# Parting dependent VectorE operations in the kernel stage of an S4 convolution, and the skip term's sum on GpSimd

## The chip, the cores and the metric

One Trainium2 chip, one of its NeuronCores. A core has five engines with a queue each: TensorE (PE, matrix products), VectorE (DVE), ScalarE (ACT), GpSimd (POOL) and SyncE (SP, which here only issues DMAs). Engines run side by side and wait for one another through semaphores. The metric is the device time of one execution in microseconds (us); lower is better.

## The reference

The model has two blocks, each run twice: a state-space convolution (S4) with a residual, and a SwiGLU feed-forward network with a residual. Length 2048, width 512, state size 128, inner width 1376, all in float32.

```python
dt = jnp.exp(log_dt)[:, None]
logdA = dt * (A_re + 1j * A_im)
dB = dt * (B_re + 1j * B_im)
P = jnp.exp(logdA[:, :, None] * l[None, None, :])      # l = 0 .. 2047
K = jnp.einsum("dn,dnl,dn->dl", Cc, P, dB).real        # convolution kernel, 512 x 2048
y = irfft(rfft(pad(K)) * rfft(pad(u)))[:L] + u * Dskip
...
x = x + S4(layernorm(x));  x = x + (silu(n @ w_gate) * (n @ w_up)) @ w_down, n = layernorm(x)
# both again, with the same weights
```

## The kernel before, in words

Work starts with the **kernel stage**: the convolution kernel K is built for 512 channels in eight chunks of 64 (`NCH = 8`, `DC = 64`). The state index lies on the 128 partitions. A lag l is written as 64 b + a, and its power as a product of two tables: `re`, `im` (the factors over a) and `g` (over b, 32 steps, with the weights C, B and dt multiplied in). PE multiplies both tables and sums over the states: these are the *lags* (`lags`, L509 and L510), 64 small products for each chunk.

For a chunk the steps are these, each written as a Python generator that yields between pieces:

- `gen_turns` (L402 to L412, VectorE): phases as integers. L402 makes those of `xz`, L406 and four L410 double up those of `im[:, 33:65]`; at the end GpSimd clears `im[:, 32]` (L412).
- `gen_trig` (ACT): sines and cosines of them, into `xz`, `re[:, 33:65]` and `im[:, 33:65]`. `gen_exp` (ACT): magnitudes, with a memset of `re[:, 0]` by GpSimd (L435). `upper` (ACT, L443): squares of `re[:, 1:32]` into `mu`.
- `gen_e` (VectorE): magnitude times phase: L457 for `im[:, :32]`, L459 for `re[:, :32]`, L461 for `im[:, 33:64]`, L464 twice for the two halves of `re[:, 33:64]`.
- `gen_g` (VectorE): L471, L475/L476 and L478/L479 make `g[0]`; then a chain of doublings for n = 1, 2, 4, 8, 16. Each is a product with the real part (L485), a product with the imaginary part into a scratch tile (L496) and their sum (L499). L496 doesn't need L485; L499 needs both; the next L485 needs L499. For n = 16 in the middle chunks L488 writes the second product into the unused half of the next chunk's `g`, and a DMA from GpSimd's queue (L489) adds it to `g` in place of L499.

After the lags ACT copies them (L520), two DMAs from SP's queue turn them around (`spread`, L527 and L529, into the tile `kt`), and `skip` (L516) adds the chunk's 64 values of Dskip to one row of `kt`, which is the skip term of the convolution. PE then takes the spectra of `kt` (`spectra`, L544, in two halves q0 = 0 and 1; ACT reads them at L563 to L568, VectorE at L572), and the result goes to DRAM as `wdr` and to the tile `w0r`. Between them PE also transforms the input's second block (L309) and sums the weights' squares (L349), which ACT makes at L346.

The tiles `re` and `im` have two buffers in turn: chunk c + 2 uses those of chunk c. `g` has two as well, `mu` and the scratch tile one.

Order: VectorE, ACT, PE and GpSimd each run their instructions in the order in which the code issues them. The first chunk's order is written out by hand (`take(gg, 1)` takes the next piece of a generator). For the others a plan holds entries `at(due, piece, n)`; it is sorted by `due`, and so gives one order for all engines. The due times are no clock: only their order counts. In period i, with start t, the plan holds `use(i, t)` (lags, copy, skip, spectra of chunk i), `factors(i + 1, t)` (`gen_g` and `gen_e` of the next chunk) and `prepare(i + 2, t)` (turns, exponentials and sines of the one after). The last chunk has an order of its own behind the plan, in which its `skip` is on GpSimd already.

After the kernel stage the convolutions by blocks (`ssm`) and the feed-forward blocks (`ffn`) follow until the end.

Of the kernel before, what the change touches and what calls it, by code (L numbers as in the profile page):

```python
# [16 lines left out]
OP = mybir.AluOpType  # L17
# [16 lines left out]
NCH = D // DC  # L34
# [41 lines left out]
def kernel(ctx, tc, x, a_re, a_im, b_re, b_im, c_re, c_im, log_dt, d_skip,  # L76
                           w_gate, w_up, w_down, c_ef, c_ei, c_ek, c_am, c_eh, c_eih, out):
    nc = tc.nc
    V, A, G, PE = nc.vector, nc.scalar, nc.gpsimd, nc.tensor
# [9 lines left out]
    def tl(shape, name, tag, dt=F32):  # L89
        return sb.tile(shape, dt, name=name, tag=tag, bufs=BUFS[tag])  # L90
# [38 lines left out]
    x1 = tl([P, 4, D], "x1", "xf")  # L129
# [70 lines left out]
    def stats(src, rows, scale, tag="stats", then=None):  # L200

        st = tl([P, 4, 6], "st", tag)
        mv = tl([P, 4, 2], "mv", tag)
        rs = tl([P, 8], "rs", tag)
        nb = rs[:, 4:]
        for r in range(rows):
            V.bn_stats(st[:, r], src[:, r])
            V.bn_aggr(mv[:, r], st[:, r])
        V.tensor_scalar(rs[:, :rows], mv[:, :rows, 1], EPS, 1.0 / scale ** 2, OP.add, OP.mult)
        G.tensor_tensor(rs[:, :rows], rs[:, :rows], mhalf[:, :rows], OP.pow)  # L210
        if then:
            then()
        V.scalar_tensor_tensor(nb[:, :rows], mv[:, :rows, 0], -1.0, rs[:, :rows], OP.mult, OP.mult)
        return rs, nb
# [160 lines left out]
    def gen_tiles(ch):  # L375
        re = tl([P, 65, DC], "re", f"W{2 * (ch % 2)}")
        im = tl([P, 65, DC], "im", f"W{2 * (ch % 2) + 1}")
        mu = tl([P, 32, DC], "mu", "n")
        xz = tl([P, 3, 5, DC], "xz", "bd")
        mz = mz2[:, ch % 2]  # L380
        return re, im, mu, xz, mz
# [70 lines left out]
    def gen_e(ts):  # L452


        re, im, mu = ts[:3]
        half = [[t.rearrange("p a (g h d) -> p a g h d", g=4, h=2)[:, :, :, o] for t in (re, mu)] for o in range(2)]
        V.tensor_tensor(im[:, :32], im[:, 64:32:-1], re[:, :32], OP.mult)  # L457
        yield
        V.tensor_tensor(re[:, :32], re[:, 64:32:-1], re[:, :32], OP.mult)  # L459
        yield  # L460
        V.scalar_tensor_tensor(im[:, 33:64], im[:, 31:0:-1], -1.0, mu[:, 1:], OP.mult, OP.mult)  # L461
        yield
        for r, u in half:
            V.tensor_tensor(r[:, 33:64], r[:, 31:0:-1], u[:, 1:], OP.mult)  # L464
            yield

    def gen_g(ch, ts, g):

        re, im, mu, xz, mz = ts
        w_ = w0[:, :, ch * DC:(ch + 1) * DC]  # L470
        V.tensor_tensor(xz, xz, mz.unsqueeze(1).to_broadcast([P, 3, 5, DC]), OP.mult)  # L471
        yield
        tmp8 = spare[0][:, :16 * DC].rearrange("p (i b d) -> p i b d", i=2, d=DC)
        tmp = tmp8
        V.tensor_tensor(g[:, :, 0], w_, re[:, 64].unsqueeze(1).to_broadcast([P, 2, DC]), OP.mult)  # L475
        V.tensor_tensor(tmp[:, :, 0], w_[:, ::-1], im[:, 64].unsqueeze(1).to_broadcast([P, 2, DC]), OP.mult)  # L476
        yield
        V.tensor_tensor(g[:, 0, 0], g[:, 0, 0], tmp[:, 0, 0], OP.subtract)  # L478
        V.tensor_tensor(g[:, 1, 0], g[:, 1, 0], tmp[:, 1, 0], OP.add)  # L479
        for n in (1, 2, 4, 8, 16):  # L480
            yield
            lv = n.bit_length() - 1
            zr = xz[:, 0:1, lv:lv + 1]
            zi = xz[:, 1:3, lv:lv + 1]
            V.tensor_tensor(g[:, :, n:2 * n], g[:, :, 0:n], zr.to_broadcast([P, 2, n, DC]), OP.mult)  # L485
            if n == 16 and 0 < ch < NCH - 1:
                tmp = gs[ch + 1][:, :, 16:32]
                V.tensor_tensor(tmp, g[:, ::-1, 0:16], xz[:, 2:0:-1, lv:lv + 1].to_broadcast([P, 2, 16, DC]), OP.mult)  # L488
                G.dma_start(g[:, :, 16:32].rearrange("p i b d -> p i (b d)"), tmp.rearrange("p i b d -> p i (b d)"),  # L489
                            accum_op=OP.add)  # L490
                continue
            step = min(n, 8)
            for b0 in range(0, n, step):
                tmp = tmp8[:, :, :step]
                o = slice(n + b0, n + b0 + step)
                V.tensor_tensor(tmp, g[:, :, b0:b0 + step], zi.to_broadcast([P, 2, step, DC]), OP.mult)  # L496
                if b0 + step == n:
                    yield
                V.tensor_tensor(g[:, :, o], g[:, :, o], tmp[:, ::-1], OP.add)  # L499
        yield  # L500

    def lags(ts, g):
        re, im = ts[:2]
# [9 lines left out]
    def skip(ch, kt, eng):  # L513

        k = kt[0:1, :, 0]
        eng.tensor_tensor(k, k, dsk[:, ch * DC:(ch + 1) * DC].rearrange("p (g d) -> p g d", g=4), OP.add)  # L516
# [120 lines left out]
    def take(it, n):  # L637
        for _ in range(n):
            next(it, None)
# [335 lines left out]
    with tc.manual_schedule(engines={mybir.EngineType.Activation, mybir.EngineType.DVE, mybir.EngineType.PE, mybir.EngineType.Pool}):  # L975
# [3 lines left out]
        def turns():  # L979
            V.tensor_tensor(rho, rho, dt, OP.mult)  # L980
            take(first, 1)
            take(ex, 14)
            take(others, 1)
            take(first, 1)
            take(gen_turns(0, ts[0]), 7)
        ft = tl([P, 2, 2, D], "ft", "ga")
        first, others = turn_units(ft, 0, DC), turn_units(ft, DC, D)
        stats_x = stats(xe, 4, 1.0, then=lambda: (turns(), take(others, 1)))
# [10 lines left out]
        gg = gen_g(0, ts[0], gs[0])  # L999
        ge, tn = gen_e(ts[0]), gen_turns(1, ts[1])  # L1000
# [2 lines left out]
        upper(ts[0])  # L1003
        take(fw[0], 1)
        take(tn, 7)
        stats_x = stats(x1, 4, 1.0, then=lambda: (take(gg, 1), take(ge, 1)))
        tr = gen_trig(ts[1])
        take(tr, 1)
        take(fw[1], 1)
        take(tr, 1)  # L1010
        for g in (gg, gg, ge, gg, gg, gg, gg, gg, gg):
            take(g, 1)
        take(fw[2], 1)
        take(fw[3], 1)
# [6 lines left out]
        for h in range(2):  # L1021
            for cp in range(2):
                nc.sync.dma_start(ndr[h, cp], x1[:, 2 * cp:2 * cp + 2, h * HD:(h + 1) * HD])
        for g in (gg, ge, gg, ge, ge):
            take(g, 1)
        for f in fw[5:]:
            take(f, 1)
# [4 lines left out]
        def at(t, f, n=1):  # L1032
            plan.append((t, len(plan), (lambda: take(f, n)) if hasattr(f, "__next__") else f))
# [5 lines left out]
        def prepare(c, t):  # L1039

            def tiles():
                ts[c] = gen_tiles(c)
            at(t + 0.05, tiles)
            steps = {k: later(lambda g=g: g(c, ts[c])) for k, g in
                     (("turns", gen_turns), ("exp", gen_exp))}
            tr = later(lambda: gen_trig(ts[c]))
            at(t + 0.35, steps["turns"])
            at(t + 0.45, tr)
            at(t + 13.0, steps["turns"], 3)
            at(t + 13.2, steps["turns"], 3)  # L1050
            at(t + 17.0, tr)
            at(t + 8.3, steps["exp"], 100)

        def factors(c, t):

            at(t + 0.2, lambda: upper(ts[c]))

            def tiles(c):
                gs[c] = tl([P, 2, 32, DC], "g", ("ga", "gb")[c % 2])
            if c == 1:  # L1060
                at(t + 0.1, lambda: tiles(c))
            if c + 1 < NCH:
                at(t + 8.05, lambda: tiles(c + 1))
            gg, ge = later(lambda: gen_g(c, ts[c], gs[c])), later(lambda: gen_e(ts[c]))
            for k in range(4):
                at(t + 0.2 + 2 * k, gg, 2)
            at(t + 0.3, ge)
            for k in range(5):
                at(t + 8.2 + k, gg)
            for k in range(4):  # L1070
                at(t + 22.0 + 0.6 * k, ge, 1 if k < 3 else 100)

        def use(c, t):

            box, kt, n = {}, kt2[:, c % 2], starts[c + 1]

            def copy():
                box["ks"] = spread_in(box["pk"])
                if c < NCH - 2:
                    spread(c, box["ks"], kt)  # L1080
            at(t, lambda: box.update(pk=lags(ts[c], gs[c])))
            at(t + 7.1, copy)
            if c == NCH - 2:
                at(t + 10.0, lambda: spread_pe(box["ks"], kt))
            at(t + 13.1, lambda: skip(c, kt, V))
            at(t + 25.0, lambda: sizes(c, kt, box["ks"]))
            for q0, ats in list(enumerate(((t + 17.5, t + 25.2, n + 2.1, n + 7.5),
                                      (n + 6.9, n + 14.0, n + 17.3, n + 21.0))))[:2 if c < NCH - 2 else 1]:
                sp = later(lambda q0=q0: spectra(c, kt, q0))
                if c == NCH - 2:  # L1090
                    tail["sp"] = sp
                    ats = ats[:2]
                for t0 in ats:
                    at(t0, sp)
# [28 lines left out]
        for i in range(NCH - 1):  # L1123
            t = starts[i]
# [5 lines left out]
            for k, t0, t1, t2, t3 in ((0, -13.0, 0.25, 13.9, 22.3), (1, 0.3, 14.5, 17.45, 22.9),  # L1130
                                      (2, 15.0, 26.5, 28.05, 36.0)):
                n = ((3, 3, 0), (3, 3, 0), (3, 3, 0), (3, 2, 0), (3, 2, 0), (3, 3, 0), (3, 3, 3))[i][k]
# [4 lines left out]
        t = starts[NCH - 1]  # L1137
# [8 lines left out]
        c, kts = NCH - 1, (kt2[:, 0], kt2[:, 1])  # L1146
# [48 lines left out]
        last = second(*sec[-1])  # L1195
# [111 lines left out]
```

## Time and profile before

| what | value |
|---|---|
| time, median of 3 runs | 1092.52 us (1089.46 to 1093.47) |
| the profiled execution | 1091.58 us, span 1089.4 us, mean granted TensorE clock 0.986 |
| busy over the span | PE 1026.5 us (94%), VectorE 969.3 (89%), ACT 547.4 (50%), GpSimd 109.6 (10%) |
| lags of the chunks, first L509 | 54.28, 83.25, 110.30, 137.28, 163.80, 191.33, 219.28, 248.48 us |
| VectorE, first operation of a chunk (L471) | 55.15, 81.49, 109.33, 136.53, 164.17, 191.77, 218.99 us (chunks 1 to 7) |

How rows are read. The timeline has start, duration, engine, line, operation, output <- input with shapes, a count, and in brackets the idle time ahead of it with what ended it. A view of windows has a stretch, its length, busy time (and instructions) of each engine, the granted clock (1.00 is full), the DMAs' busy share and GB/s. The view of a line gives min/median/max durations in ns. All times are from the span's start.

### The profile page before, as it was taken

To read this page: it belongs to the slowest core of one execution; us is meant where nothing else is said; L and a number is where in the kernel's file an instruction comes from. 1 tells how busy PE (TensorE), PEld (TensorE's weight loads), DVE (VectorE), ACT (ScalarE), POOL (GpSimd) and SP (SyncE) were. 2 spreads that over 40 slices of the span, in tenths; PEclk is the share of its full clock that TensorE was granted. 3 is DMA by queue.
4 is the path that set the end of the run, shared out by engine and by line. 5 is a ranking of instruction groups with operands and counts; after the bars stand their busy time and mean duration, and the time that the engine had idled before them with its cause. 6 is when DMAs were issued, how large, how long until landed. Compare 5 with 4: busy or idle time off the path is not lost.

```text
span 1089.4 us, 22811 instructions
## 1 busy us (share of the span) xinstructions
PE 1026.5 (94%) x9302; PEld 810.9 (74%) x9302; DVE 969.3 (89%) x1405; ACT 547.4 (50%) x1093; POOL 109.6 (10%) x163
## 2 busy tenths in 40 slices
PE   1989999998779999999999999999999999999998
PEld 1868888887677777686779676786867687686775
DVE  8999999998999999999999989999998999993221
ACT  6989998953367162466462253533425432134211
POOL 1112222220002010012010001201100000000000
PEclk9989999998989999999999999999999999999999
DMA  5366777768765356342444553443545245312000
GB/s 212 108 180 167 173 166 179 187 181 272 234 182 172 120 145 215 105 141 68 131 117 133 158 160 130 119 136 100 166 126 180 59 127 147 109 61 63 2 25 20
DMA packets 125003, 149.23 MB, mean 137 GB/s; under 512 B 50897, under 2 KB 75985, under 8 KB 124130
## 3 DMA queue, kind: packets, MB, share of 16 engines
q1 hardware_dynamic: 112994, 122.27, 36.8%
q0 software_dynamic: 11904, 25.50, 10.0%
q8 instruction: 73, 1.20, 0.5%
q14 instruction: 32, 0.26, 0.1%
HBM read 97.66 MB, written 33.82 MB: 121 GB/s over the span
## 4 chain that ended last, share of the span: by engine, by line
PE 27%; DVE 27%; issue 11%; DMA 5%; ACT 3%; POOL 1%; SPq 0%; DVEq 0%; POOLq 0%; ACTq 0%
PE pgu L930 5%; PE pgu L931 5%; PE pgu L933 5%; DVE t L812 4%; DVE yk L815 4%; PE py L948 3%; PE py L946 3%; PE py L947 3%; DVE yk L812 3%; PE pi L784 2%; DVE sg L937 2%; DVE hl L939 2%; DMA n<-xdr 1%; DVE yl L232 1%; DMA mix<-nn 1%
## 5 line engine op out<-in xcount | busy, mean ns | idle before, releaser
L930 PE MATMUL pgu<-mix,wsl 128*128 128x256 f16 x1280 | 298.6, 273 | 5.4 <-DVE sg L937 2.1
L931 PE MATMUL pgu<-mix,wsl 128*128 128x256 f16 x1280 | 298.4, 273 | 0.0
L933 PE MATMUL pgu<-mix,wsl 128*128 128x256 f16 x1280 | 194.8, 273 | 0.0
L931 PEld LDWEIGHTS <-wsl 128*128 128x128 f16 x1280 | 125.2, 98 | 22.5 <-issue 6.7
L933 PEld LDWEIGHTS <-wsl 128*128 128x128 f16 x1280 | 125.2, 98 | 18.4 <-issue 3.8
L930 PEld LDWEIGHTS <-wsl 128*128 128x128 f16 x1280 | 125.2, 98 | 16.4 <-issue 1.2
L946 PE MATMUL py<-wsl,hh 128*128 128x512 f16 (+1 forms) x352 | 134.2, 381 | 0.1
L948 PE MATMUL py<-wsl,hl 128*128 128x512 f16 (+1 forms) x352 | 133.5, 381 | 0.1
L947 PE MATMUL py<-wsl,hh 128*128 128x512 f16 x320 | 121.8, 381 | 0.0
L815 DVE TENSOR_TENSOR yk<-yk,t 128x1024 f32<-128x1024 f32 x96 | 116.9, 1218 | 0.5
L812 DVE TENSOR_TENSOR t<-uu,w 128x1024 f32<-128x1024 f32 x96 | 117.0, 1218 | 0.3
L938 ACT ACTIVATE hh<-sg 128x512 f16<-128x512 f32 x80 | 50.1, 627 | 114.0 <-DVE sg L937 114.0
L544 PE MATMUL pw<-kt,ek 128*128 128x256 f32 (+1 forms) x384 | 93.2, 381 | 0.0
L937 DVE SCALAR_TENSOR_TENSOR sg<-pgu,sc,sg 128x512 f32<-128x512 f32 x80 | 59.6, 745 | 37.7 <-ACT sg L936 37.6
L936 ACT ACTIVATE sg<-pgu,sc 128x512 f32<-128x512 f32 x80 | 54.2, 678 | 70.7 <-PE pgu L933 66.9
L544 PEld LDWEIGHTS pw<-kt,ek 128*128 128x128 f32 x384 | 74.8, 199 | 8.8
L939 DVE TENSOR_TENSOR hl<-sg,hh 128x512 f16<-128x512 f32 x80 | 54.8, 685 | 15.3 <-ACT hh L938 15.3
L227 POOL TENSOR_TENSOR rs<-mv,mhalf 128x2 f32<-128x2 f32 (+1 forms) x21 | 33.6, 1598 | 336.3 <-ACT mv L226 296.3
L509 PE MATMUL pk<-re,g 128*32 128x64 f32 x1024 | 65.0, 317 | 2.2 <-DMA g<-g 1.9
L948 PEld LDWEIGHTS <-hl 128*128 128x128 f16 (+1 forms) x352 | 34.4, 98 | 39.2 <-issue 0.8
L947 PEld LDWEIGHTS <-hh 128*128 128x128 f16 (+1 forms) x352 | 34.6, 98 | 38.4 <-issue 0.8
L510 PE MATMUL pk<-im,g 128*32 128x64 f32 x1024 | 63.1, 301 | 0.0
(265 smaller groups left out, 2010.1 us busy)
## 6 DMA issues: line engine op xcount, KB each, us to landing
uu<-udr SPq DMA_DIRECT2D x96, 256.0 KB, 3.0
w<-wdr SPq DMA_DIRECT2D x96, 256.0 KB, 2.8
g<-g POOLq DMA_DIRECT2D x6, 1024.0 KB, 9.2
udr<-fu POOLq DMA_DIRECT2D x22, 256.0 KB, 2.7
udr<-u SPq DMA_DIRECT2D x16, 256.0 KB, 3.3
n<-xdr SPq DMA_DIRECT2D x4, 1024.0 KB, 6.4
kdr<-ks SPq DMA_DIRECT2D x6, 512.0 KB, 2.9
kt<-kdr SPq DMA_DIRECT2D x24, 128.0 KB, 3.0
```

The costliest lines, as they stand in the source:

```text
L509: PE.matmul(o, lhsT=g[:, 0, :, d], rhs=re[:, 0:64, d], start=True, stop=False, tile_position=(0, 32 * grp))
L544: PE.matmul(pw[:, i], lhsT=e, rhs=kt[:, :, c + 4 * k0:4 * k1:4, :].rearrange("p g k d -> p k g d"), start=c == 0, stop=c == 3)
L812: V.tensor_tensor(t, uu.unsqueeze(2).to_broadcast([P, NQ, 2, 2, DC]), w.unsqueeze(3).to_broadcast([P, NQ, 2, 2, DC]), OP.mult)
L815: V.tensor_tensor(yk, yk, t, OP.add)
L930: PE.matmul(o, lhsT=wgu(wi, k, 0)[:, fs], rhs=nh[:, k], start=k == 0, stop=False)
L931: PE.matmul(o, lhsT=wgu(wi, k, 1)[:, fs], rhs=nh[:, k], start=False, stop=False)
L933: PE.matmul(o, lhsT=wgu(wi, k, 0)[:, fs], rhs=nlo[:, k], start=False, stop=k == 3)
L937: V.scalar_tensor_tensor(sg, pgu[:, 1], sc6[:, 4:5], sg, OP.mult, OP.mult)
L939: V.tensor_tensor(hl[:, f0:f0 + 2], sg, hh[:, f0:f0 + 2], OP.subtract)
L946: PE.matmul(py[r], lhsT=hh[:n, f, rc], rhs=wd(f, 0)[:n], start=f == 0, stop=False)
L947: PE.matmul(py[r], lhsT=hh[:n, f, rc], rhs=wd(f, 1)[:n], start=False, stop=False)
L948: PE.matmul(py[r], lhsT=hl[:n, f, rc], rhs=wd(f, 0)[:n], start=False, stop=f == FT - 1)
```

## The change

It gives the pieces of the kernel stage another order. `stats` issues the next row's `bn_stats` ahead of a row's `bn_aggr`. `gen_e` puts the first L464 ahead of L461. `gen_g` yields between L496 and L499 at every n, and between L485 and L488 at n = 16. The prologue's order and the plan's due times are set anew: in a middle chunk L459 goes from the end of the period to its front; the steps for n = 1 and 2 are drawn together; the steps for n = 4, 8 and 16 go behind due time 12.9 and alternate with L406 and the four L410, which stood behind L488; so L488 and its DMA come after them. `skip` of chunks 0 to 6 goes from VectorE to GpSimd at the same due time.

```diff
@@ stats
-        for r in range(rows):
-            V.bn_stats(st[:, r], src[:, r])
-            V.bn_aggr(mv[:, r], st[:, r])
+        for r in range(rows + 1):
+            if r < rows:
+                V.bn_stats(st[:, r], src[:, r])
+            if r:
+                V.bn_aggr(mv[:, r - 1], st[:, r - 1])
@@ gen_e
+        V.tensor_tensor(half[0][0][:, 33:64], half[0][0][:, 31:0:-1], half[0][1][:, 1:], OP.mult)
+        yield
         V.scalar_tensor_tensor(im[:, 33:64], im[:, 31:0:-1], -1.0, mu[:, 1:], OP.mult, OP.mult)
         yield
-        for r, u in half:
-            V.tensor_tensor(r[:, 33:64], r[:, 31:0:-1], u[:, 1:], OP.mult)
-            yield
+        V.tensor_tensor(half[1][0][:, 33:64], half[1][0][:, 31:0:-1], half[1][1][:, 1:], OP.mult)
+        yield
@@ gen_g
+        yield
         for n in (1, 2, 4, 8, 16):
-            yield
             ...
             V.tensor_tensor(g[:, :, n:2 * n], g[:, :, 0:n], zr.to_broadcast([P, 2, n, DC]), OP.mult)
             if n == 16 and 0 < ch < NCH - 1:
+                yield
                 tmp = gs[ch + 1][:, :, 16:32]
                 V.tensor_tensor(tmp, g[:, ::-1, 0:16], ...)
                 G.dma_start(g[:, :, 16:32]..., tmp..., accum_op=OP.add)
+                yield
                 continue
             for b0 in range(0, n, step):
+                if n == 16:
+                    yield
                 ...
                 V.tensor_tensor(tmp, g[:, :, b0:b0 + step], zi.to_broadcast([P, 2, step, DC]), OP.mult)
-                if b0 + step == n:
-                    yield
+                yield
                 V.tensor_tensor(g[:, :, o], g[:, :, o], tmp[:, ::-1], OP.add)
-        yield
+            yield
@@ the prologue
-        stats_x = stats(x1, 4, 1.0, then=lambda: (take(gg, 1), take(ge, 1)))
+        stats_x = stats(x1, 4, 1.0, then=lambda: (take(gg, 1), take(ge, 1), take(gg, 1)))
-        for g in (gg, gg, ge, gg, gg, gg, gg, gg, gg):
+        for g in (gg, gg, ge, gg, gg, ge, gg, gg, gg):
-        for g in (gg, ge, gg, ge, ge):
+        for g in (gg, gg, gg, ge, gg, gg, ge, ge):
@@ prepare
-            at(t + 13.0, steps["turns"], 3)
-            at(t + 13.2, steps["turns"], 3)
+            for d, n in ((13.0, 1), (13.04, 1), (13.08, 1), (13.12, 1), (13.16, 2)):
+                at(t + d, steps["turns"], n)
@@ factors
-            for k in range(4):
-                at(t + 0.2 + 2 * k, gg, 2)
-            at(t + 0.3, ge)
-            for k in range(5):
-                at(t + 8.2 + k, gg)
-            for k in range(4):
-                at(t + 22.0 + 0.6 * k, ge, 1 if k < 3 else 100)
+            last = c == NCH - 1
+            for d in (0.2, 0.25, 2.2, 2.25, 2.35, 2.4, 2.6, 8.2, 8.4, 9.2, 10.2, 10.3, 11.2, 11.4, 11.6, 11.8) if last else \
+                    (0.2, 0.25, 2.2, 2.3, 2.4, 2.5, 2.6, 12.9, 13.02, 13.06, 13.1, 13.14, 13.2):
+                at(t + d, gg)
+            for d in (0.3, 2.3, 8.3, 10.1, 11.3) if last else (0.3, 2.25, 22.0, 23.7, 23.8):
+                at(t + d, ge)
@@ use
-            at(t + 13.1, lambda: skip(c, kt, V))
+            at(t + 13.1, lambda: skip(c, kt, G))
```

## The prediction

> **What bounds the kernel now.** I read the page's forty slices first: TensorE (PE) and VectorE (DVE) are both at nine tenths in the slices from 27 to 246 us, which is the stage the edit touches. So I took the busy time of each engine there, in five stretches of 27 us:
>
> ```profile
> core 0: us, PE busy (x) PEld busy (x) DVE busy (x) ACT busy (x) POOL busy (x), PEclk, DMA share, GB/s
> 83.00:110.00 27.00, 27.00 (x344) 23.82 (x342) 26.59 (x32) 25.54 (x56) 7.51 (x11) 1.00 0.67 169
> ...
> 191.00:218.00 27.00, 26.67 (x342) 23.77 (x342) 26.59 (x33) 24.44 (x56) 7.56 (x11) 1.00 0.79 185
> sum 135.00, PE 134.33 PEld 118.95 DVE 132.94 ACT 123.30 POOL 36.61; mean PE 26.87 PEld 23.79 DVE 26.59 ACT 24.66 POOL 7.32
> ```
>
> PE is idle for 0.67 us in 135, VectorE for 2.06. The two run abreast, so what shortens VectorE alone can win at most PE's idle time. Next, VectorE's timeline of one chunk:
>
> ```profile
> 55.15 1.17 DVE L471 TENSOR_TENSOR xz<-xz,mz 128x960 f32<-128x960 f32 x1
> ...
> 136.53 1.18 DVE L471 TENSOR_TENSOR xz<-xz,mz 128x960 f32<-128x960 f32 x1
> ...
> 140.68 0.96 DVE L572 TENSOR_TENSOR wo<-pw,wo 128x768 f32<-128x768 f32 x1
> 141.54 0.22 DVE L478 TENSOR_TENSOR g<-g,spare 128x64 f32<-128x64 f32 x1
> ...
> 141.93 0.31 DVE L485 TENSOR_TENSOR g<-g,xz 128x128 f32<-128x128 f32 x1
> ...
> 144.08 0.71 DVE L485 TENSOR_TENSOR g<-g,xz 128x512 f32<-128x512 f32 x1
> 144.70 0.70 DVE L496 TENSOR_TENSOR spare<-g,xz 128x512 f32<-128x512 f32 x1
> 145.43 0.69 DVE L499 TENSOR_TENSOR g<-g,spare 128x512 f32<-128x512 f32 x1
> 146.16 1.23 DVE L485 TENSOR_TENSOR g<-g,xz 128x1024 f32<-128x1024 f32 x1
> 147.30 1.22 DVE L496 TENSOR_TENSOR spare<-g,xz 128x1024 f32<-128x1024 f32 x1
> ...
> 149.82 2.29 DVE L485 TENSOR_TENSOR g<-g,xz 128x2048 f32<-128x2048 f32 x1
> 152.02 2.29 DVE L488 TENSOR_TENSOR g<-g,xz 128x2048 f32<-128x2048 f32 x1
> 154.23 0.29 DVE L406 TENSOR_TENSOR im<-tdk,am 128x128 int32<-128x128 int32 x1
> 154.55 0.75 DVE L410 CUSTOM_DVE_ANT_0 im<-im 128x256 uint16<-128x256 uint16 x2
> 155.22 0.21 DVE L516 TENSOR_TENSOR kt<-kt,tdk 1x64 f32<-1x64 f32 x1
> 155.35 1.94 DVE L410 CUSTOM_DVE_ANT_0 im<-im 128x1024 uint16<-128x1024 uint16 x2
> 157.20 2.28 DVE L459 TENSOR_TENSOR re<-re 128x2048 f32<-128x2048 f32 x1
> ...
> 159.83 2.21 DVE L461 SCALAR_TENSOR_TENSOR im<-im,mu 128x1984 f32<-128x1984 f32 x1
> ...
> 164.17 1.16 DVE L471 TENSOR_TENSOR xz<-xz,mz 128x960 f32<-128x960 f32 x1
> ```
>
> Subtract starts. L485 and L496 of 512 elements don't need each other: 144.70-144.08 = 0.62 for 0.71 of work, an overlap of 0.09. L499 needs L496: 145.43-144.70 = 0.73 for 0.70, a gap of 0.03. A needed predecessor right ahead costs about 0.115 us. Then who holds the chunk's end and its start, from the timelines of PE, GpSimd (POOL) and the view of the line L489:
>
> ```profile
> 62.73 0.15 POOL L435 MEMSET re<- 128x64 f32 x1 [2.66 <-issue]
> 83.25 0.49 PE L509 MATMUL pk<-re,g 128*32 128x64 f32 x8
> 110.30 0.50 PE L509 MATMUL pk<-re,g 128*32 128x64 f32 x8
> 118.17 0.49 PE L510 MATMUL pk<-im,g 128*32 128x64 f32 x7
> 118.76 0.15 POOL L435 MEMSET re<- 128x64 f32 x1 [2.09 <-issue]
> 127.40 1.24 POOL L489 DMA_DIRECT2D g<-g  x1 [8.49 <-DVE im L406]
> 137.28 0.50 PE L509 MATMUL pk<-re,g 128*32 128x64 f32 x8 [0.27 <-DMA g<-g]
> 182.22 1.24 POOL L489 DMA_DIRECT2D g<-g  x1 [9.45 <-DVE im L406]
> 191.33 0.51 PE L509 MATMUL pk<-re,g 128*32 128x64 f32 x8 [0.40 <-DMA g<-g]
> 219.28 0.51 PE L509 MATMUL pk<-re,g 128*32 128x64 f32 x8 [1.22 <-DMA g<-g]
> DMA to landing us min/median/max: 8.8/9.2/10.0
> ```
>
> The lags of chunk c (L509/L510) take 118.66-110.30 = 8.4 us. They wait for the accumulating DMA g<-g, which follows L488: in three chunks PE already waits for it (0.27, 0.40, 1.22). And chunk c+2 uses chunk c's re and im buffers: GpSimd's first write to the new re, L435, comes 0.1 after the lags' last record. L406 is the first write to the new im, so it is bound in the same way; today it comes late enough (154.23 in a chunk whose lags began at 137.28) never to wait.
>
> **The change, part by part.** *Hand-offs.* In a middle chunk VectorE's order becomes: L471, L475, L476, L457, L402, L572, L478, L479, L459, the steps for n = 1 and 2, L485 and L496 for n = 4, then L406, L499, L410, L485 and L496 (n = 8), L410, L499, L410, L485 (n = 16), L410, L488 with its DMA, and L464, L461, L464. Eight needed neighbours are parted (L479 to L485; within and after n = 4 and n = 8; three in the turns), which is 8 x 0.115 = 0.92, and L516 leaves VectorE (155.35-155.22 = 0.13): 1.05 us of 27.2. In the prologue some five hand-offs go, statistics included: 0.5. In the last chunk five and L516: 0.7. That would be 7.5 us if VectorE alone were the bound.
>
> *L406 and the turns go from behind L488 to the middle of the g steps, and L488 with its DMA goes late.* Here a wait is added. L406 must now follow the lags of the chunk two before, and behind it in VectorE's queue stand the rest of the g steps and L488. From L406 to L488's end, by the starts above: L406 0.20, L499 0.61, L485 and L496 2 x 1.14, L499 1.14, the four L410 about 2.35 (157.20-154.55 less L516 and two hand-offs, and rounded up for the overlap), L485 2.20, L488 2.29: 11.1 us. So there is a closed loop, lags to lags:
>
> lags 8.4 + release 0.1 + VectorE 11.1 + from L488's end (152.02+2.29 and alike in every chunk) to the issue 0.3 + from issue to the next L509 9.5 (137.28-127.40 = 9.88, 191.33-182.22 = 9.11) = 29.4 us.
>
> The rows name L406 as the issue's releaser, since it ended last; in the code the issue asks only for L488. Were it tied to the instruction behind L488, that would now be L464 (half of L459's work), some 0.9 more per turn.
>
> Today lags follow lags every (219.28-83.25)/5 = 27.2 us. VectorE reaches L406 before it is released: from L488's end it has L464, L461, L464 (164.17-159.83 = 4.34) and, in the next chunk, 10.9 us to L406 (141.93-136.53 = 5.4, less a hand-off, with L459's 2.2 in it, 144.70-141.93 = 2.8 and 0.61): 15.2 us, against 0.3+9.5+8.4+0.1 = 18.3. So VectorE stands idle for about 3 us ahead of each L406, though it has less to do; PE has 27.2-8.4 = 18.8 us of other work between lags and stands idle for about 2.2.
>
> *The first chunk of the loop.* VectorE starts at 55.15-0.5 = 54.65. L406 comes 10.9-0.86 (no L572 yet; 141.54-140.68) later, at 64.7, when the first lags (L435 at 62.73) are over. L488 ends at 75.8, and the lags follow at 75.8+0.3+9.5 = 85.6 instead of 83.25: +2.35. Five turns of the loop, each 2.2 longer, bring the sixth chunk's lags to 232.6 instead of 219.28: +13.3.
>
> *L459 to the front, L464 and L461 in another order.* L459 now overwrites what ACT's L443 reads, so it can wait for ACT at the start of a chunk. That lies inside VectorE's 3 us of spare time: taken as nothing; without that cover it costs what L443 is late, some tenths per chunk.
>
> *The skip term on GpSimd.* Its only run there in this trace, and what feeds it:
>
> ```profile
> L516 POOL TENSOR_TENSOR kt<-kt,tdk x1: 553/553/553, 261.3 to 261.3; 1x64 f32<-1x64 f32 x1
> 122.44 1.74 SPq L529 DMA_DIRECT2D kt<-kdr  x4
> ```
>
> It waits for kt: issued until 124.18, and 3.0 to land by the page's DMA issues, so 127.2, or 8.5 after the lags; with 0.55 it ends 9.1 after them. Behind it in GpSimd's queue stand the memset of im and the g<-g issue, which isn't ready before 11.1+0.3; and PE wants kt at 11.5 (another half spectrum and a block of the input come first). Both cover it: nothing. Were kt 2.5 late, each further us would enter the loop. Against this speaks the Trainium skill, "SBUF — State Buffer", section "Who interferes with whom": a VectorE instruction with two SBUF inputs and a GpSimd instruction that reads SBUF shut each other out for a whole instruction. By it the sum could need kt one 2.3 us instruction later, still about the cover; the row's 0.55 us, taken while VectorE was working, does not show such a block.
>
> *After the stage.* From the sixth chunk's lags PE works without a gap to those of the last, and VectorE then waits for what follows:
>
> ```profile
> 248.48 0.49 PE L509 MATMUL pk<-re,g 128*32 128x64 f32 x8
> 250.45 0.97 DVE L572 TENSOR_TENSOR wo<-pw,wo 128x768 f32<-128x768 f32 x1 [2.31 <-ACT w0r L568]
> ```
>
> PE's 29.2 us between 219.28 and 248.48 stay, so the last lags come at 261.8. VectorE's own end of the stage, at about 253, is ahead of that; it then waits at L572 until PE has delivered. Both engines enter the rest 13.3 later, and I see nothing there that gives time back.
>
> **The sum.** The profiled execution took 1091.58 us (span 1089.4). 1091.6 + 13.3 = 1104.9. The median of the runs is 0.9 above that execution; I leave it for what the tail may absorb, and say 1105. Its own bounds: with issue to L509 at 8.8 and at 10.1 the loop takes 28.7 and 30.0, the first shift is 1.7 and 3.0, in all 9 and 17: 1100 to 1110.
>
> **The rivals.** *PE falls to half clock.* PE would be idle for 2 to 3 us once per chunk. Two short waits in one place show that this can be enough:
>
> ```profile
> 258.15 1.93 PE L536 MATMUL kp<-ks,ident 128*32 128x256 f32 x32 [1.25 <-ACT ks L520]
> 261.88 0.66 PE L589 MATMUL pw<-kt,ef 128*128 128x64 f32 x4 [1.79 <-POOL kt L516]
> 263.50:270.00 6.50, 6.50 (x27) 0.50 1.05 397
> ```
>
> After idle times of 1.25 and 1.79 the granted clock is 0.50 for 6.5 us. No lags in the trace ran at that clock. If they take twice their time for 6.5 us, each of six loses 3.25: +19.5, 1125; if they are paced by issue and not by the clock, nothing. In between, 1115. The Trainium skill, "TensorE: Matmul & The Clock Gate", section "What's actually happening", says that the clock falls after at least one idle window of about 3.4 us. By that rule waits of 2 to 3 us cost nothing and the sum stays; the row is against it, since two shorter ones did it here.
>
> *The loop does not close.* If g<-g reached PE in under 27.2-8.4-0.1-11.1-0.3 = 7.3 us, PE's own work would bind again and the time would be about 1092. None of six landed in under 8.8. Some of this case also holds a shift that the tail takes back.
>
> *VectorE alone was the bound, and PE's records hide waits.* They are modelled at their ends, so PE could be paced by VectorE while it looks full. Then the hand-offs pay in full, 1092.5-7.5 = 1085, provided that the DMA is in under 7.3 as well, or is taken off the loop. Against it: PE's records follow one another at the same intervals in every chunk, with named waits of 0.27 to 1.22.
>
> **How the numbers follow.** The loop as summed 0.56 (1100 to 1110), with half clock on top 0.19 (1110 to 1125), no loop 0.16 (1089 to 1096), VectorE's full gain 0.09 (1084 to 1087). About 0.5% is what a measurement of this kernel can tell from no change, 5.5 us. The range 1089 to 1120 leaves out the last case and the top of the half clock.
>
> **What the changed profile would show.** Right: L406 idle ahead of it for about 3 us with PE's L510 as releaser; L509 waits of 2 us and more for g<-g in chunks 2 to 6; lags 29.4 apart; VectorE's share lower in the third to the ninth slice; L516 on GpSimd at about 0.6 with no wait of PE on it. Wrong: L406 without a wait, lags 27 apart or less, or a landing under 8 us; or L516 blocked for whole VectorE instructions with L489 late behind it.

## The result, and the profile after

| kernel | median | ratio to before, 95% | first gate matmul | from there to the span's end |
|---|---|---|---|---|
| before | 1092.72 us (4 runs beside the changed kernel) | | 300.46 us | 788.9 us |
| changed | 1119.44 us (1115.23 to 1120.44) | 1.0246 [1.0217, 1.0274] | 337.59 us | 779.8 us |

The change costs 26.7 us. The forecast was 1105: slower, but by half as much. The first gate matmul is the first product of the first feed-forward block; it splits the span (1089.4 and 1117.4 us) into the kernel stage with what hangs on it, and the rest. By this mark the stage loses 37.1 us and the rest wins 9.1. The prediction had 13.3 and nothing. One kernel below, with the skip sum alone on GpSimd, also had three executions of 1344 to 4339 us at a granted clock of 0.75 to 0.24; its median is that of the other seven.

The changed kernel's lines lie a little lower: L488 was L485, L492 was L488, L493 the g<-g issue (L489), L408 and L412 the turns (L406 and L410), L515 and L516 the lags (L509 and L510), L522 the skip sum (L516), L550 the spectra (L544). The same stretches as before, in the view of windows:

```profile
core 0: us, PE busy (x) PEld busy (x) DVE busy (x) ACT busy (x) POOL busy (x), PEclk, DMA share, GB/s
83.00:110.00 27.00, 25.76 (x328) 22.74 (x329) 15.62 (x24) 16.56 (x46) 7.59 (x11) 0.92 0.60 155
...
137.00:164.00 27.00, 21.78 (x271) 18.80 (x270) 18.45 (x19) 19.74 (x34) 16.37 (x10) 0.87 0.65 141
...
sum 135.00, PE 119.28 PEld 103.64 DVE 106.96 ACT 101.33 POOL 57.40; mean PE 23.86 PEld 20.73 DVE 21.39 ACT 20.27 POOL 11.48
```

PE and VectorE both stand idle now (busy for 119.28 and 106.96 us of 135, against 134.33 and 132.94 before); GpSimd alone has more time than before, 57.40 against 36.61. Its instruction is the skip sum; the view of its line, with who waited for it:

```profile
L522 POOL TENSOR_TENSOR kt<-kt,tdk x8: 601/6315/14194, 70.0 to 296.0; 1x64 f32<-1x64 f32 x8
...
  PE pw L550: 25.9, 6
```

Sixty-four additions take from 0.6 to 14.2 us, and PE waits six times for them, 25.9 us in all. Now GpSimd's timeline, then VectorE's over the first of these sums and a later one:

```profile
69.99 14.19 POOL L522 TENSOR_TENSOR kt<-kt,tdk 1x64 f32<-1x64 f32 x1 [6.45 <-DMA kt<-kdr]
84.22 0.78 POOL L493 DMA_DIRECT2D g<-g  x1
107.87 6.48 POOL L522 TENSOR_TENSOR kt<-kt,tdk 1x64 f32<-1x64 f32 x1 [6.20 <-DMA kt<-kdr]
114.40 0.77 POOL L493 DMA_DIRECT2D g<-g  x1
138.24 9.99 POOL L522 TENSOR_TENSOR kt<-kt,tdk 1x64 f32<-1x64 f32 x1 [6.39 <-DMA kt<-kdr]
148.28 0.77 POOL L493 DMA_DIRECT2D g<-g  x1
```

```profile
69.98 2.29 DVE L488 TENSOR_TENSOR g<-g,xz 128x2048 f32<-128x2048 f32 x1
72.18 1.22 DVE L412 CUSTOM_DVE_ANT_0 im<-im 128x2048 uint16<-128x2048 uint16 x1
73.31 2.29 DVE L492 TENSOR_TENSOR g<-g,xz 128x2048 f32<-128x2048 f32 x1
75.52 1.19 DVE L463 TENSOR_TENSOR re<-re,mu 128x992 f32<-128x992 f32 x1
...
83.53 0.49 DVE L404 TENSOR_TENSOR xz<-th,am 128x320 int32<-128x320 int32 x1
...
112.99 1.19 DVE L463 TENSOR_TENSOR re<-re,mu 128x992 f32<-128x992 f32 x1
114.09 0.69 DVE L354 TENSOR_REDUCE cmx<-nrm 128x1 f32<-128x512 f32 x1
```

The first sum starts 0.01 after L488, a product of two SBUF tiles, and ends at 84.18, 0.16 after VectorE's last operation ahead of its pause (83.53 + 0.49). From L488 to that last operation VectorE runs eleven without a pause, and each starts up to 0.1 before the one ahead of it has ended: 72.18 against 69.98 + 2.29 = 72.27, 75.52 against 73.31 + 2.29 = 75.60. The second sum ends at 114.35, in the middle of L354, a reduction whose one input (`nrm`, a sum of PE's) lies in PSUM. The g<-g issue stands behind the sum in GpSimd's queue and leaves 0.04 after it (84.18 to 84.22), though L492 ended at 75.60. So the delay reaches PE twice, through kt and through g:

```profile
84.24 1.22 PE L550 MATMUL pw<-kt,ef 128*128 128x256 f32 x2 [11.43 <-POOL kt L522]
123.27 0.50 PE L515 MATMUL pk<-re,g 128*32 128x64 f32 x8 [1.69 <-DMA g<-g]
148.29 1.22 PE L550 MATMUL pw<-kt,ef 128*128 128x256 f32 x2 [5.22 <-POOL kt L522]
```

### The profile page after: what moved, and what is told of

It is laid out like the page before. It is cut to its first block, busy times and chain, and to the rows that moved or that the text cites. A ratio compares the mean times of both kernels' runs of the same rounds, so it can differ in the third digit from the quotient of the medians.

```text
span 1117.4 us, 22818 instructions
## 1 busy us (share of the span) xinstructions
PE 1031.1 (92%) x9302; PEld 813.7 (73%) x9302; DVE 962.8 (86%) x1398; ACT 546.4 (49%) x1093; POOL 153.1 (14%) x170
## 4 chain that ended last, share of the span: by engine, by line
PE 38%; DVE 29%; issue 12%; DMA 12%; ACT 4%; POOL 4%; SPq 1%; DVEq 0%; POOLq 0%; ACTq 0%
PE pgu L939 4%; PE pgu L936 4%; PE pgu L937 4%; DVE t L818 4%; DVE yk L821 4%; PE pw L550 4%; PE pf L311 3%; POOL kt L522 3%; DMA g<-g 3%; PE pk L515 3%; PE py L952 3%; PE py L954 3%; PE py L953 3%; DVE yk L818 3%; PE pk L516 3%
## 5 line engine op out<-in xcount | busy, mean ns | idle before, releaser
L550 PE MATMUL pw<-kt,ek 128*128 128x256 f32 (+1 forms) x384 | 95.1, 386 | 0.0
L550 PEld LDWEIGHTS pw<-kt,ek 128*128 128x128 f32 x384 | 76.2, 202 | 9.3
L515 PE MATMUL pk<-re,g 128*32 128x64 f32 x1024 | 65.8, 317 | 7.0 <-DMA g<-g 5.5
L550 PE MATMUL pw<-kt,ef 128*128 128x256 f32 (+1 forms) x128 | 41.4, 407 | 30.4 <-POOL kt L522 25.9
L229 POOL TENSOR_TENSOR rs<-mv,mhalf 128x2 f32<-128x2 f32 (+1 forms) x21 | 28.4, 1350 | 289.2 <-ACT mv L228 289.1
L516 PE MATMUL pk<-im,g 128*32 128x64 f32 x1024 | 63.9, 302 | 0.0
```

The lines of the kernel that those rows point to most:

```text
L515: PE.matmul(o, lhsT=g[:, 0, :, d], rhs=re[:, 0:64, d], start=True, stop=False, tile_position=(0, 32 * grp))
L516: PE.matmul(o, lhsT=g[:, 1, :, d], rhs=im[:, 0:64, d], start=False, stop=True, tile_position=(0, 32 * grp))
L550: PE.matmul(pw[:, i], lhsT=e, rhs=kt[:, :, c + 4 * k0:4 * k1:4, :].rearrange("p g k d -> p k g d"), start=c == 0, stop=c == 3)
```

## The experiments

Each was run beside the kernel before; ratios are to its runs.

**The skip sum back on VectorE, at its place in the plan**

```diff
-            at(t + 13.1, lambda: skip(c, kt, G))
+            at(t + 13.1, lambda: skip(c, kt, V))
```

> The changed order as it is, the skip term's sum back on VectorE (L516's old engine). Theory A (shut out): GpSimd's small sum, 6 to 14 us long in the changed kernel, is kept waiting by VectorE's unbroken run of operations with two SBUF inputs, and PE and the accumulating DMA wait behind it; with the sum on VectorE only the loop of the prediction is left: 1105 by its sum, 1092 to 1097 if VectorE's spare time swallows it. Theory B (the loop with half clock): the order itself makes the time, the long record of the sum is only a wait that would be there anyway: 1112 to 1119.

Measured: 1120.2 us, 1.0265 [1.0244, 1.0287]; the gate matmul at 331.56. Both theories had less. The sum takes 0.2 us again, but the time does not come back. The view of its line and PE's waits:

```profile
L522 DVE TENSOR_TENSOR kt<-kt,tdk x7: 204/212/214, 69.1 to 269.8; 1x64 f32<-1x64 f32 x7
...
  DMA kt<-kdr: 15.4, 6
```

```profile
PE pk L515 <- DMA g<-g: 32.0, 6, 6.4
```

VectorE now stands 15.4 us for kt with L488, L492 and their DMA behind the sum, and the lags come some 32 us apart (85.95, 118.01, ... 181.97). In the changed order this place in the plan is too early for VectorE, which has to stand there until kt lands, so this run could not part a shut-out from a mere wait. At the mark it does win 6.0 us, and the rest, which fell back to its old order (below), takes it away again.

**The skip sum alone on GpSimd, in the order before**

```diff
-            at(t + 13.1, lambda: skip(c, kt, V))
+            at(t + 13.1, lambda: skip(c, kt, G))
```

> The kernel before, with only the skip term's sum moved to GpSimd; the order stays. Theory A: the old order has twelve hand-offs per chunk at which VectorE's pipe runs empty for 0.03 us; if they let GpSimd in, the sum takes under 3 us and the time is 1092 to 1095; if they don't, it lasts until VectorE next waits or reduces from PSUM, PE stands still for 5 us and more per chunk, and the time is 1110 to 1125. Theory B: 1092, the sum takes 0.6.

Measured: 1091.14 us, 0.9996 [0.9983, 1.0008], the same time. Both theories allow it, so this run does not part them. The view of the line, and the first sum beside what VectorE runs:

```profile
L516 POOL TENSOR_TENSOR kt<-kt,tdk x8: 727/816/1230, 73.3 to 261.6; 1x64 f32<-1x64 f32 x8
```

```profile
72.41 2.74 DVE L410 CUSTOM_DVE_ANT_0 im<-im 128x256 uint16<-128x256 uint16 x4
...
73.26 0.79 POOL L516 TENSOR_TENSOR kt<-kt,tdk 1x64 f32<-1x64 f32 x1
```

On the same engine, from 0.7 to 1.2 us: GpSimd is not slow at it. What differs is what VectorE runs beside it: here the sum falls among the four L410, each of which needs the one ahead.

**The changed kernel with small breaks in VectorE's run**

```diff
+    pad = sb.tile([P, 1], F32, name="pad")
...
+            for d in (13.05, 13.11, 13.15, 13.17, 13.21):
+                at(t + d, lambda: V.memset(pad, 0.0))
```

> The changed kernel with five tiny VectorE memsets (one column, no input) between the steps from n = 8 on, where kt lands. Theory A: the sum ends within 0.5 us of the first memset behind kt's landing, so it lasts at most 3 us, and the time falls to within 3 us of the kernel with the sum on VectorE. Theory B: nothing changes, 1119.

Measured: 1094.93 us, 1.0039 [1.0017, 1.0062]. Five added instructions per chunk win 2.07% of the changed kernel's 2.46%, that is 22.6 us of 26.7 (by the two intervals, some 4 us either way). The view of the sum's line, the first sum with the memset at which it ends, PE's timeline at the lags, what L409 (L406 before) waits for, and the landing of g<-g from the view of its line:

```profile
L523 POOL TENSOR_TENSOR kt<-kt,tdk x8: 710/1142/2410, 70.0 to 272.1; 1x64 f32<-1x64 f32 x8
```

```profile
69.97 2.41 POOL L523 TENSOR_TENSOR kt<-kt,tdk 1x64 f32<-1x64 f32 x1 [6.44 <-DMA kt<-kdr]
...
72.16 0.06 DVE L1093 MEMSET pad<- 128x1 f32 x1
```

```profile
85.07 0.47 PE L516 MATMUL pk<-re,g 128*32 128x64 f32 x8 [3.14 <-DVE wo L579]
113.39 0.50 PE L516 MATMUL pk<-re,g 128*32 128x64 f32 x8 [2.34 <-DMA g<-g]
...
231.21 0.50 PE L516 MATMUL pk<-re,g 128*32 128x64 f32 x8 [2.48 <-DMA g<-g]
```

```profile
  PE pk L517: 10.5, 5
```

```profile
DMA to landing us min/median/max: 8.9/9.2/9.4
```

Each of the six sums in the middle chunks ends 0.2 us after the start of a memset, here at 72.38, and what is left is the predicted loop: (231.21 - 85.07)/5 = 29.2 us from lags to lags (single turns 28.3 to 31.4), where the prediction had 29.4. L409 now waits for the lags in five chunks, 10.5 us in all, and PE waits for g<-g; where its row names L579 instead, as at 85.07, that ended last by the profile, and the g<-g issued at 75.99 lands about then (8.9 to 9.4 later). The gate matmul comes at 311.26, 10.8 after that of before and 26.3 ahead of that of the changed kernel, near PE's 25.9 us of waits for the sum.

**What lets GpSimd in: two small programs**

```python
G.tensor_tensor(k, f, a1, OP.add)            # 1x64, the skip sum's shape
for i in range(14):                          # beside it, one form for each case
    V.tensor_tensor(o[:, i], a, b, OP.mult)  # 128x1024, no one needs the one before
```

> A small program in place of the kernel: nothing of the reference is computed. Six stretches; in each VectorE runs 14 operations without a wait while one GpSimd operation on 1x64 elements becomes ready after the first: 14 sums of 1024 elements from SBUF that don't need one another; 14 that each need the one before; 14 reductions (one SBUF input); 14 products with one input from PSUM; the first kind with a GpSimd memset, which reads nothing; the first kind with one tiny VectorE memset after the fifth. Theory A: GpSimd's operation lasts to the end of the 14 (about 16 us) in the first stretch, under 1 us in the third, fourth and fifth, about 6 us in the sixth; in the second it shows whether the 0.03 us between needed operations are enough. Theory B: about 0.6 us in all.

> A second small program, nothing of the reference: six times a run of 14 VectorE sums from SBUF that don't need one another, each with one break behind the fifth, and one GpSimd sum ready at the start. Breaks: one sum that needs its forerunner; a reduction (one input); a product with one input from PSUM; two tiny memsets, the second waiting for the first; one tiny memset waiting for the fifth sum; a product with a constant (one input). Theory A, sharpened by the first small program (16.0 us beside sums that need nothing, 1.2 where each needs the one before, 0.3 beside one input from SBUF): any break at which VectorE's second SBUF input pauses lets GpSimd in, so 6 to 7 us in all six. Rival: only a break that empties VectorE's pipe (the needed sum and the two waiting memsets) does so, and the others give 16.

(The two texts call VectorE's products sums.) GpSimd's timeline of the first program; k_free stands beside independent products of two SBUF tiles, k_needed beside products that each need the one before, k_single beside reductions, k_psum beside products with one input in PSUM; f_clear is a memset of GpSimd's, and k_padded has one tiny memset, which waits for nothing, behind VectorE's fifth product:

```profile
7.40 15.99 POOL L50 TENSOR_TENSOR k_free<-f_free,a 1x64 f32<-1x64 f32 x1 [6.95 <-DVE f_free L47]
23.85 1.23 POOL L50 TENSOR_TENSOR k_needed<-f_needed,a 1x64 f32<-1x64 f32 x1 [0.46 <-DVE f_needed L47]
41.62 0.31 POOL L50 TENSOR_TENSOR k_single<-f_single,a 1x64 f32<-1x64 f32 x1 [16.54 <-DVE f_single L47]
57.66 0.31 POOL L50 TENSOR_TENSOR k_psum<-f_psum,a 1x64 f32<-1x64 f32 x1 [15.73 <-DVE f_psum L47]
66.53 0.14 POOL L50 MEMSET f_clear<- 1x64 f32 x1 [8.55 <-DVE small L49]
82.70 15.99 POOL L50 TENSOR_TENSOR k_padded<-f_padded,a 1x64 f32<-1x64 f32 x1 [16.04 <-DVE f_padded L47]
```

VectorE's timeline beside the first two:

```profile
7.25 15.96 DVE L59 TENSOR_TENSOR o<-a,b 128x1024 f32<-128x1024 f32 x14
...
23.70 17.59 DVE L53 TENSOR_TENSOR o<-o,b 128x1024 f32<-128x1024 f32 x14
```

The sum waits out all fourteen independent products (15.99 beside 15.96), and only one of the needed ones (1.23). In the second program VectorE's run has one break, behind five products:

```profile
7.38 5.77 POOL L48 TENSOR_TENSOR k_needed_once<-f_needed_once,a 1x64 f32<-1x64 f32 x1 [6.94 <-DVE f_needed_once L47]
23.67 5.78 POOL L48 TENSOR_TENSOR k_reduce_once<-f_reduce_once,a 1x64 f32<-1x64 f32 x1 [10.52 <-DVE f_reduce_once L47]
...
88.03 15.46 POOL L48 TENSOR_TENSOR k_scalar_once<-f_scalar_once,a 1x64 f32<-1x64 f32 x1 [10.52 <-DVE f_scalar_once L47]
```

One needed product or one reduction is enough: the sum ends right there. So it did, at 5.78, with a product from PSUM, with a tiny memset that waits for the operation ahead of it and with two tiny memsets, the second of which needs the first. A product with a constant, one SBUF input, 0.68 us for 1024 elements, does not let it in (15.46). Theory A so missed twice, at k_padded (about 6 us forecast) and at the constant (6 to 7); its rival of the second program, that only an emptied pipe lets GpSimd in, is out by the reduction and the product from PSUM. Each case was measured once. One thing stays open: the memsets in the kernel above need only an earlier memset that is long done, and they let the sum in, while the one of k_padded, which waits for nothing either, did not.

**The turns' first step and the g steps laid out anew, the sum on VectorE**

```diff
-            at(t + 0.35, steps["turns"])
+            at(t + 2.25, steps["turns"])
...
-            for d, n in ((13.0, 1), (13.04, 1), (13.08, 1), (13.12, 1), (13.16, 2)):
+            for d, n in ((13.0, 1), (13.12, 1), (13.16, 1), (13.24, 1), (13.28, 2)):
...
-                    (0.2, 0.25, 2.2, 2.3, 2.4, 2.5, 2.6, 12.9, 13.02, 13.06, 13.1, 13.14, 13.2):
+                    (0.2, 0.25, 2.2, 2.3, 4.2, 4.3, 6.2, 6.3, 8.2, 9.2, 13.1, 13.14, 13.2):
...
-            for d in (0.3, 2.3, 8.3, 10.1, 11.3) if last else (0.3, 2.25, 22.0, 23.7, 23.8):
+            for d in (0.3, 2.3, 8.3, 10.1, 11.3) if last else (0.3, 21.9, 22.0, 23.7, 23.8):
...
-            at(t + 13.1, lambda: skip(c, kt, G))
+            at(t + 13.26, lambda: skip(c, kt, V))
```

> The hand-offs parted in another way: the n = 1, 2 and 4 steps and the position of L459 as before the change; L406 and the four L410 between the steps from n = 8 on, so that L488 and its DMA come 0.4 us later than before and L406 to L488 is 6.4 us; the skip term on VectorE, behind L488. Loop theory: lags to lags by the loop is 8.4+0.1+6.4+0.3+9.3 = 24.5, below PE's 27.0, so no wait at L406, lags 27.0 to 27.3 apart; the first gate matmul of the feed-forward blocks at 298 to 302; by the later part of the kernel before (786 to 789 us from there) 1089 to 1092, by that of the changed kernel (780 to 781) 1081 to 1085. Rival, that the lags in the changed order are slow for another reason than L406's wait: 29 apart, gate at 311, 1092 to 1095.

Measured: 1087.49 us, 0.9965 [0.9952, 0.9977]. The lags come at 82.06, 109.11, ... 217.33: 27.05 apart and no longer bound by the loop, since of the g steps only the sum for n = 8, and n = 16 with L492, stand behind L408. The gate matmul comes at 301.63, as the loop theory had it; with the new order of the rest the time lies 2.5 us above the 1081 to 1085 of the text.

**The turns behind L492 and its DMA**

```diff
-            for d, n in ((13.0, 1), (13.04, 1), (13.08, 1), (13.12, 1), (13.16, 2)):
+            for d, n in ((13.3, 3), (13.5, 3)):
...
-            at(t + 13.1, lambda: skip(c, kt, G))
+            at(t + 13.4, lambda: skip(c, kt, V))
```

> The changed order, but L406 and the four L410 behind L488 and its DMA again, and the skip term on VectorE between them. The loop through L406 is undone; L459 stays in front, so L488 ends some 2 us later in its chunk than before the change. Loop theory: one shift of about 2 us and lags 27.0 to 27.3 apart, gate at 300 to 304, 1082 to 1093 by the later part. Rival: lags 29 apart as in the changed order without the shut-out, gate at 311.

Measured: 1106.51 us, 1.0135 [1.0118, 1.0153]: my theory missed. With the turns out of the loop the lags still come 29.5 us apart ((201.72 - 83.55)/4). ACT's and VectorE's waits in this kernel:

```profile
ACT re L424 <- DVE im L412: 25.6, 6, 4.8
```

```profile
DVE g L478 <- ACT re L426: 9.3, 6, 1.8
```

ACT's sines wait for the late L412, and the next chunk's L478 waits for the sines, since the product that was L459 (L461 now, 2.3 us) no longer stands between the last turns and L478. By these waits the turns have a latest place as well as an earliest, and the loop that I had drawn was not the only one; no run tests this reading.

**The sum on GpSimd in that layout**

```diff
-            at(t + 13.26, lambda: skip(c, kt, V))
+            at(t + 13.1, lambda: skip(c, kt, G))
```

> The same as the kernel with the turns in the middle and the skip term on VectorE, but the sum on GpSimd, where kt lands in a run of VectorE operations that need nothing of their neighbours. Theory A: the sum lasts to the next break of that run, 5 to 15 us, PE waits for it, and the time is 15 to 30 us above the other's. Rival, that only the changed kernel's own order did it: under 2 us, no difference.

> The same kernel as e8_mid_g, timed: the turns' steps moved to the middle of the chain, hand-offs parted, the skip term's sum on GpSimd. One look gave 1083.7 with sums of 0.6 to 3.2 us on GpSimd and a wait of PE of 1.1 us in all. Expected: 1083 to 1087, that is 2 to 4 us under the same kernel with the sum on VectorE (1087.5), since VectorE loses 0.2 us of sum and its wait for the skip term's transfer per chunk. Rival (a single look says nothing at this size): 1087 to 1089.

Measured: 1083.67 us in a single run and 1083.26 over four, 0.9908 [0.9887, 0.9929]. Theory A of the first text missed: it had 5 to 15 us a sum, and the sums took 0.6 to 3.4. VectorE's timeline, and GpSimd's row beside it, from the second of these:

```profile
123.18 2.29 DVE L492 TENSOR_TENSOR g<-g,xz 128x2048 f32<-128x2048 f32 x1
125.38 1.95 DVE L412 CUSTOM_DVE_ANT_0 im<-im 128x1024 uint16<-128x1024 uint16 x2
```

```profile
122.83 3.40 POOL L522 TENSOR_TENSOR kt<-kt,tdk 1x64 f32<-1x64 f32 x1 [6.23 <-DMA kt<-kdr]
```

The sum ends at 126.23, inside the pair of L412, where the second needs the first. This is the fastest kernel here, and it has the sum on GpSimd: where VectorE has a break in time (all six sums of the middle chunks end in that pair), the move is harmless. Over the stats part alone (0.9933 [0.9912, 0.9955], below) its gain is not certain, since the intervals overlap. It is 4.2 us under the same layout with the sum on VectorE (there the intervals do not overlap). The 0.2 us of VectorE's time per sum make 1.4 of that; where the rest comes from is open.

**Where the rest gave time back**

The feed-forward part is ordered by an automatic scheduler, and it comes in two orders. From the first gate matmul on, the traces of the two kernels record 6321 matmuls each, and at 2613 places of this row another line of the code stands in the changed kernel than in the kernel before. Each of the other kernels differs from one of these two at no more than 296 places. Of the kernels run, those with the order before took 786.0 to 790.2 us from the first gate matmul to the end of the span (before and four others, mean 787.9), those with the new one 779.8 to 784.6 (seven, mean 782.0). The part of the change that tips it in the three pairs below is `stats`:

```diff
-        for r in range(rows):
-            V.bn_stats(st[:, r], src[:, r])
-            V.bn_aggr(mv[:, r], st[:, r])
+        for r in range(rows + 1):
+            if r < rows:
+                V.bn_stats(st[:, r], src[:, r])
+            if r:
+                V.bn_aggr(mv[:, r - 1], st[:, r - 1])
```

> The kernel before with one part of the change alone: stats takes each row's aggregation behind the next row's statistics. The factors' chain and the skip term stand as before. Compared instruction by instruction with the kernel before, it keeps the order through the loop of chunks, and from the first gate matmuls on it has the order of matmuls that the changed kernel has there and the kernel before has not. Theory (the later part's order gives time back): the gate matmuls start near 300, as before, and from there to the span's end it takes 780 to 785 us, as in the changed kernel, instead of 789: 1083 to 1088. Rival (the shorter rest of the changed kernel comes from starting late, or from other cores of the change): 1090 to 1093, rest 787 to 790.

> The changed kernel with only its part in stats undone: rows' statistics and aggregation alternate again. The factors' chain and the skip term on GpSimd stand as changed; compared instruction by instruction, its part from the first gate matmuls on has the order of the kernel before. Theory (the later part's order gives time back): gate matmuls near 337.6 as in the changed kernel, then 786 to 789 us instead of 780: 1124 to 1128. Rival (the rest is shorter because it starts late, whatever its order): 1119 to 1121.

> The kernel of e6_turns_mid with only the part in stats undone, so that its part from the first gate matmuls on has the order of the kernel before. Theory: gate matmuls near 301.6 as in e6, then 786 to 789 instead of 781.5: 1091 to 1095, so that parting the factors' chain, with the turns in its middle, is worth nothing and all of e6's gain over the kernel before is the later part's order. Rival (the gain is the parted chain's): 1087 to 1089.

| base | without the stats part | with it | difference |
|---|---|---|---|
| before | 1092.69 (gate 300.46, rest 788.9) | 1085.89 (300.20, 780.4) | -6.8 |
| changed | 1126.2 (335.59, 787.7) | 1119.44 (337.59, 779.8) | -6.8 |
| turns in the middle | 1094.12 (302.00, 790.2) | 1087.49 (301.63, 781.5) | -6.6 |

Ratios to before: 0.9933 [0.9912, 0.9955], 1.031 [1.0284, 1.0336] and 1.0022 [1.0005, 1.0038] for the three new kernels. The gate matmuls' rows, of the kernel before and of the one with stats alone:

```profile
300.46 0.27 PE L930 MATMUL pgu<-mix,wsl 128*128 128x256 f16 x1 [1.11 <-ACT mix L869]
```

```profile
300.20 0.27 PE L932 MATMUL pgu<-mix,wsl 128*128 128x256 f16 x1 [1.11 <-ACT mix L871]
```

They start together, and the whole gain lies behind them. So some 6.7 us hang on the stats part, wherever it is made (by the ratios to before 7.3, 7.0 and 6.2). Its own hand-offs are not the reason by what one kernel shows: the first experiment has the stats part and yet the order before, and its rest took 786.9 us, like the others of that order. Why the new order is faster was not followed further. Without the stats part the layout with the turns in the middle is no faster than the kernel before (1.0022): as a whole, with the hand-offs that it parts, it wins nothing.

## Why the prediction was wrong, by its own steps

**The skip term: "Both cover it: nothing".** This step failed, and it is larger than the whole miss of 14: +22.6 us. The cover was counted from a sum of 0.55 us, at most one 2.3 us instruction later. The sums took up to 14.2, and the prediction's own sign of being wrong, L516 blocked with the g<-g issue late behind it, came. The rule that the prediction weighed, in the Trainium skill, "SBUF — State Buffer", "Who interferes with whom", names the right pair: a VectorE instruction with two SBUF inputs and a GpSimd one that reads SBUF. The traces agree with it on reductions, PSUM inputs and a memset by GpSimd, which do not clash (0.31, 0.31, 0.14 us). On its length the measurement decides otherwise: a block of one whole instruction would be 1.2 us in the small program, and it was 15.99, as long as VectorE's run had no break. The row of 0.55 us was no evidence against a block: that sum ended at 261.82, 0.17 behind VectorE's L680 (260.72 and 0.93 long), so it may itself have been a short wait. What let it in there is not known; in the kernel before the sums mostly meet breaks (0.7 to 1.2 us with all eight on GpSimd). The two parts of the change work against each other: the gap of 0.03 us at a needed neighbour, which the first part removes, is what would let the second part in.

**The hand-offs.** The price was right: 14 needed products take (17.59 - 15.96)/14 = 0.116 us more each, and the prediction had 0.115. That VectorE's gain alone does not pay was right too.

**The loop.** Right in place and nearly in size: with the sums let in, 29.2 us from lags to lags against 29.4, the seventh lags at 231.21 against 232.6, g<-g landing in 8.9 to 9.4. By the mark it costs 10.8 us instead of 13.3: the first shift was 1.8 (85.07 - 83.25) for 2.35, and each turn 2.0 longer for 2.2. L408's waits are 5.6 us in three in the changed kernel, not 3 in every chunk, because there the late sum sets the pace.

**L459 at the front: nothing.** Held: its counterpart L461 waits 3.9 us for ACT in six chunks, the "tenths per chunk" that were to be covered. In the kernel with breaks they are, since VectorE waits at L409 behind them all the same.

**After the stage: "nothing there that gives time back".** Failed: behind the mark 9.1 us come back, some 6.7 of them by the automatic order; the other 2.4 are open.

**The half clock.** Two windows of the changed kernel, the granted clock in the third column from the end:

```profile
78.00:84.00 6.00, 0.00 (x0) 0.00 (x0) 6.00 (x7) 2.94 (x3) 6.00 (x1) 0.50 0.11 44
84.00:90.00 6.00, 5.76 (x19) 4.86 (x20) 0.02 (x1) 1.15 (x2) 2.70 (x6) 0.71 0.96 182
```

It came (0.50, then 0.71, behind PE's wait of 11.43 us), but it met spectra, not lags: the first eight spectra took 87.68 - 84.24 = 3.44 us, the next eight 89.41 - 87.68 = 1.73, so it cost 1.7 there, and about as much behind the waits at 148.29 and 244.83. This is part of the 22.6. In the kernel with breaks the waits of 2.3 to 3.1 us ahead of the lags came as forecast, and in four of the six chunks the lags then ran for 2 to 3 us at a granted clock of 0.50. Two windows of the lags from 85.07 on, at half and at full clock:

```profile
85.10:87.30 2.20, 2.20 (x82) 2.20 (x85) 2.20 (x3) 1.53 (x3) 0.61 (x2) 0.50 0.84 322
88.00:90.20 2.20, 2.20 (x91) 2.20 (x85) 2.10 (x6) 1.36 (x4) 0.51 (x1) 1.00 0.90 286
```

In both, a group of eight L516 starts every 0.44 us. So the rival's condition came true, with shorter waits than 3.2 us, but not its price: these lags do not slow with the clock, and its 19.5 us did not come.

**The sum again.** Shut-out +22.6, order of the rest -6.8; what is left for the loop is 26.7 - 22.6 + 6.8 = +10.9. This last term is a remainder and carries the 4 us of doubt of the first; that it meets the mark's 10.8 so closely is luck. At the mark itself the sum is 26.3 for the shut-out and 10.8 for the loop, 37.1 together, and 9.1 come back behind it.

## What to carry to other kernels

An operation that reads SBUF on GpSimd is priced by what VectorE runs when its inputs land: the time to VectorE's next break, not GpSimd's own duration; taking out VectorE's hand-offs takes out these breaks. Look also at what is queued behind such an operation, here a DMA issue on which the next chunk hung. And split the time at a mark behind the edited stage before crediting the edit: a part that a scheduler orders can change by several us through an edit elsewhere.

## What the runs showed of the hardware

GpSimd's read of SBUF was shut out for as long as VectorE ran products of two SBUF tiles without a break: 15.99 us over 14 products, and 14.19 in the kernel. What ended it: an operation that needs the one ahead (1.23), one with an input in PSUM or a reduction (0.31 each beside a run of these, 5.77 to 5.78 as a single break behind five products), a tiny memset that waits, and in the kernel a memset that needs only an earlier one (each sum ended 0.2 us after its start). What did not end it: a tiny memset without a wait in the small program (15.99) and a product with a constant at 0.68 us (15.46). In the kernel L412 did not end it either where its forerunner was done 2 us before (72.18 in the first sum above); both of its inputs come from im, though the view names the tile once. The lags kept their pace, eight in 0.44 us, at a granted clock of 0.50 as at 1.00; the spectra took twice their time (3.44 against 1.73 us for eight). What decides in the hardware between the two engines is not settled by these runs.
